# Decay row broadcast by its load, the gate kept on one partition, and a reordered schedule, in a fused RWKV and mixture-of-experts kernel

## The chip, the cores and the metric

The kernel runs on one core of one Trainium2 chip. The metric is the device time of one execution in microseconds (us); the time before is the median of three executions. Engine names in the trace: PE is TensorE's matrix multiplication, PEld its weight load, DVE is VectorE, ACT is ScalarE, POOL is GpSimd, SP is SyncE, which issues most DMAs.

## The reference

Two steps follow each other. The first is a linear attention with a decaying state, over 4 batches, 8 heads, 768 positions and a head size of 48. The second sends each whole batch through one of 8 experts.

```
# attention, for each batch and head
for t in range(S):
    y[t] = r[t] @ (state + (u*k[t])[:, None] * v[t][None, :])
    state = w[:, None] * state + k[t][:, None] * v[t][None, :]
# experts: x is y with the heads side by side, [4, 768, 384]
logits = x.mean(axis=1) @ w_gate                  # [4, 8]
e = argmax(logits); gate = softmax(logits)[e]
out[b] = gate[b] * (relu(x[b] @ w1[e[b]]) @ w2[e[b]])   # 384 -> 1024 -> 384
```

## The kernel before

The sequence is cut into blocks of 256 positions, three to a batch, so that blocks 0 to 11 cover the four batches. Instead of stepping through positions, k and r of a block are multiplied by powers of the decay (tiles `dk` and `dr`, made once at the start from `w` by a logarithm and four exponentials), and the rest is matrix products.

All the work is written as one list of tokens, ORDER. A loop at the end calls the function `do_<letter>` for each token, and each engine runs its instructions in the order in which the tokens name them. `X.2@4` means step X of block 2 in PSUM bank 4; a letter behind a slash is the engine (A for ACT, V for DVE, P for POOL, X for a product that DVE makes straight out of PSUM). Nothing is reordered at run time: an instruction that waits holds up all that stands behind it on its engine. The steps:

- L loads k, r or v of a block (on SP's queue; loads of block 7 stand back for the first part of the expert weights, those of block 8 for a later part). K and R multiply k and r by the decay, V casts v to bf16. Block 0 has K and R in two halves, the first of which is `q`.
- T transposes k and r on PE, E copies them out of PSUM, P multiplies the two (the term with u), U sums that product over a head, `v` (and `t`, a copy for POOL) multiplies it with v.
- A forms the scores on PE, G masks them on DVE (four times a block, 128x512 each). y, Y and J add the three parts of the output in PSUM: from the state, from the scores, and from the term with u.
- S adds a half block to the state in PSUM, Z decays the state, s copies it to SBUF.
- N copies the output, X transposes it for the experts (and sums it for the mean, `p`; from block 5 on `x` sums it), x copies it.
- The gate, once a batch: g (sum), l (logits on PE), m (maximum and its index on DVE), e and w (softmax), i (the index is read into a register of POOL), a and b (DMAs of the chosen expert's w1 and w2, issued by POOL).
- M and H are the first expert product and its ReLU, O and o the second and its scaling by the gate, B the store.
- `W.i.m` issues m products of 128x512 zeros that nothing reads: fillers.

Before the loop stand the load of the decay row (L129), the loads of block 0, memsets and masks. The decay row is loaded as one row on one partition; c.ln takes its logarithm there, into row 0 of a tile of zeros (`lnrow`); `cB` multiplies this tile on PE by `first`, which is one on row 0 and zero elsewhere, so that the row stands on all partitions of a PSUM bank; c.dk and c.dr (L234) make the exponentials from there. In the gate, l (L582) hands PE a column of the sums broadcast to 128x128 as the stationary operand, so that the logits stand on all partitions, and m, e and w run on 128 partitions.

S has two forms. In one (L468) it makes 16 products with 64x64 stationary operands, in the other (L477) 8 with 64x128; the former is used from block 3 on, save for the first half of a batch.

Of the kernel before, what the change touches and what calls it, by code (L numbers as in the profile page):

```python
# [757 lines left out]
```

## Time and profile before

| | |
|---|---|
| three executions | 130.01, 130.10, 130.91 us (median 130.1) |
| the profiled execution | 129.35 us, of which 127.7 us from the first to the last instruction |
| PE busy | 120.0 us |
| DVE busy | 84.7 us |
| ACT busy | 78.1 us |
| POOL busy | 78.0 us |
| HBM | 26.76 MB read, 4.72 MB written |

How to read it: the span runs from the first to the last instruction, and the time of the execution is 1.65 us longer. The profiled execution was 0.75 us shorter than the median. A share of busy time is a mean over stretches with different limits; in this kernel the stretch up to about 36 us has no expert work, and the rest has.

### The profile page before, as it was taken

The page shows a single profiled execution, that of the slowest core. Times are in us where ns is not written, and L with a number is a line of the kernel's source. Part 1 is how long each engine was busy: PE and PEld are TensorE (multiplying, and loading weights), DVE is VectorE, ACT ScalarE, POOL GpSimd, SP SyncE. Part 2 cuts the span into 40 slices and gives each one's busy share as a digit, 9 for nine tenths or more (in the row PEclk, how much of TensorE's full clock was granted, in tenths as well). Part 3 has the DMA queues.
Part 4 walks back from the last instruction along what each step waited for, and adds up shares of the span by engine and source line. Part 5 has one row for each costly group of instructions (what it writes and reads, how often), then busy time and mean ns, then how long its engine had stood idle before and what let it go on. Part 6 is the DMA issues. An engine that isn't in the chain of part 4 may idle for free.

```text
span 127.7 us, 4933 instructions
## 1 busy us (share of the span) xinstructions
PE 120.0 (94%) x2103; PEld 82.1 (64%) x2107; DVE 84.7 (66%) x192; ACT 78.1 (61%) x192; POOL 78.0 (61%) x72
## 2 busy tenths in 40 slices
...
GB/s 28 324 320 325 322 234 314 189 243 270 129 139 276 224 161 232 277 258 236 229 270 280 273 224 90 62 185 197 64 0 0 9 174 202 240 400 211 0 257 115
DMA packets 47768, 25.50 MB, mean 200 GB/s; under 512 B 38401, under 2 KB 46338, under 8 KB 47746
## 3 DMA queue, kind: packets, MB, share of 16 engines
...
q8 instruction: 16, 0.26, 0.8%
q14 instruction: 6, 0.05, 0.1%
HBM read 26.76 MB, written 4.72 MB: 246 GB/s over the span
## 4 chain that ended last, share of the span: by engine, by line
PE 91%; ACT 2%; DVE 2%; issue 2%; ACTq 0%
PE hp L648 25%; PE op L683 24%; PE y L500 8%; PE at L439 5%; PE wp L219 5%; PE tp L325 4%; PE tp L338 3%; PE xp L538 3%; PE s L468 3%; PE s L477 2%; PE lgp L582 2%; PE y L425 2%; PE u L399 2%; PE lnb L226 1%; PE op L673 1%
## 5 line engine op out<-in xcount | busy, mean ns | idle before, releaser
L648 PE MATMUL hp<-xt,w 128*128 128x384 bf16 x192 | 36.3, 326 | 0.0
L683 PE MATMUL op<-w,ht 128*128 128x384 bf16 x184 | 33.7, 326 | 0.0
L449 DVE TENSOR_TENSOR gt<-at,mask 128x512 bf16<-128x512 f32 x48 | 31.0, 683 | 3.8 <-PE at L439 3.5
L663 DVE TENSOR_SCALAR ht<-hp 128x384 bf16<-128x384 f32 x30 | 16.0, 552 | 13.3 <-PE hp L648 13.3
L683 PEld LDWEIGHTS <-ht 128*128 128x128 bf16 x184 | 17.4, 99 | 10.8 <-issue 0.2
L648 PEld LDWEIGHTS <-w 128*128 128x128 bf16 x192 | 17.4, 98 | 10.3 <-issue 0.3
L294 POOL TENSOR_TENSOR kp<-k,dk 128x768 bf16<-128x768 f32 x11 | 20.0, 1818 | 2.7 <-DMA k<-in_k_dram 2.1
L661 ACT ACTIVATE ht<-hp 128x384 bf16<-128x384 f32 x34 | 15.5, 501 | 9.4 <-PE hp L648 9.4
L294 POOL TENSOR_TENSOR rp<-r,dr 128x768 bf16<-128x768 f32 x11 | 20.0, 1814 | 1.6 <-DMA r<-in_r_dram 1.5
L704 ACT ACTIVATE ob<-op,gw 128x384 f32<-128x384 f32 (+1 forms) x17 | 9.5, 576 | 13.1 <-PE op L683 11.0
L627 POOL DMA_DIRECT2D w<-in_moe_w_dram x9 | 7.2, 797 | 15.7 <-issue 10.4
L365 ACT COPY tw<-tp 128x1024 bf16<-128x1024 bf16 x12 | 12.2, 1016 | 5.2 <-PE tp L338 4.6
L389 POOL TENSOR_TENSOR prod<-tw 128x1024 bf16<-128x1024 bf16 x6 | 12.7, 2121 | 1.8 <-DVE tw L363 1.8
L210 ACT CAST xn<-y 128x384 bf16<-128x384 f32 x22 | 9.7, 486 | 5.6 <-PE y L425 5.6
L706 DVE TENSOR_SCALAR ob<-op,gw 128x384 f32<-128x384 f32 (+1 forms) x8 | 4.6, 590 | 11.4 <-PE op L683 8.0
L495 ACT CAST st<-s 64x192 bf16<-64x192 f32 x32 | 10.1, 314 | 3.5 <-PE s L477 2.2
L219 PE MATMUL wp<-zeros 128*128 128x512 bf16 x30 | 9.0, 413 | 1.5 <-DVE zeros L135 1.4
L439 PE MATMUL at<-tw 64*64 64x128 bf16 x384 | 9.7, 219 | 0.4 <-DVE tw L363 0.2
L559 ACT ACTIVATE xt<-xp 128x256 bf16<-128x256 bf16 x21 | 7.8, 391 | 3.1 <-PE xp L538 3.1
L210 ACT CAST vb<-v 128x768 bf16<-128x768 f32 x10 | 8.4, 840 | 1.5 <-DMA v<-in_v_dram 1.5
L363 DVE COPY tw<-tp 128x512 uint32<-128x512 uint32 x12 | 8.1, 687 | 1.7 <-PE tp L338 0.8
L416 DVE TENSOR_TENSOR vt<-vb,u 128x768 bf16<-128x768 bf16 x8 | 7.6, 947 | 1.6 <-PE u L399 1.6
...
## 6 DMA issues: line engine op xcount, KB each, us to landing
w<-in_moe_w_dram POOLq DMA_DIRECT2D x15, 384.0 KB, 6.5
k<-in_k_dram SPq DMA_DIRECT2D x12, 384.0 KB, 5.2
r<-in_r_dram SPq DMA_DIRECT2D x12, 384.0 KB, 5.4
v<-in_v_dram SPq DMA_DIRECT2D x12, 384.0 KB, 5.9
out_dram<-ob SPq DMA_DIRECT2D x11, 384.0 KB, 6.9
w<-in_moe_w_dram POOLq DMA_DIRECT2D x2, 192.0 KB, 4.6
...
out_dram<-ob SPq DMA_DIRECT2D x1, 192.0 KB, 2.2
```

The lines of the kernel that those rows point to most:

```text
L210: nc.scalar.copy(out, in_)
L219: nc.tensor.matmul(out=wp, lhsT=zeros[:, 0:128], rhs=zeros, start=True, stop=True)
L294: e.tensor_mul(dst[n % NR].rearrange("p (g a) d -> p a g d", a=2)[:, :, :, 0:D], *(t.rearrange("p (a q) j d -> p a (q j) d", a=2) for t in ...
L365: nc.scalar.copy(out, in_)
L389: e.tensor_mul(prod.rearrange("x g c p -> x c g p"), tk, tw[:, :, 1].rearrange("x c q j p -> x c (q j) p"))
L439: nc.tensor.matmul(out=at[a][64 * c : 64 * c + 64, 128 * q : 128 * q + 128], lhsT=tw[rows, c, 0, q, j, :], rhs=tw[rows, c, 1, q].rearrange ...
L449: nc.vector.tensor_mul(gts[n][:, j, a], ats[n, j][a].rearrange("x (q s) -> x q s", q=NQ), mask[:, j].rearrange("x j p -> x (j p)").unsquee ...
L500: nc.tensor.matmul(out=out, lhsT=lhsT, rhs=rhs, start=(n, c) not in begun, stop=False, skip_group_check=True)
L648: nc.tensor.matmul(out=hp[:, 0:SB], lhsT=wts[b][1][i][:, ct, 128 * f : 128 * f + 128], rhs=xts[b][:, ct, SB * sb : SB * sb + SB], start=(c ...
L661: nc.scalar.activation(out=o, in_=hp[:, 0:SB], func=ACT.Relu)
L663: nc.vector.tensor_scalar_max(o, hp[:, 0:SB], 0.0)
L683: nc.tensor.matmul(out=op[:, 0:DM], lhsT=hts[b, half][:, f, 128 * si : 128 * si + 128], rhs=wts[b][2][half][:, f, :], start=(half == 0 and ...
```

## The change

The row of the decay is loaded with a DMA that reads it 128 times, once for each partition, and the logarithm is taken on all of them (`lnw`); `cB` and the memset of `lnrow` are gone, and c.dk and c.dr read SBUF. The logits are formed on one partition; m, e and w run there, and m reads PSUM without a copy. Two new steps bring the gate's weight to all partitions: f, a product on PE of a row of ones with the weight, and h, a copy of its result. S and J take their form from a letter in the token: Q is the form with small stationary operands, H for J writes 128 columns. `ident` becomes the middle of a tile with zeros on both sides.

ORDER is new as a whole. 47 fillers stand in it instead of 34, of which 34 instead of 20 follow the first transpose of block 0. Many copies change their engine: of `v` 11 are on DVE instead of 8 (and the copy `t` is gone), of N 6 instead of 2, of s 8 instead of 4, of o 10 instead of 8, of x 3 instead of 1, of E 13 instead of 12, of H 24 instead of 30; POOL casts five v instead of two. S is in its 16-product form 11 times instead of 12. Loads are spread over the list; on SP's queue only the gate's matrix (cg), the order within some blocks and the stores move.

The list up to the first expert product, and from l.3 to the first product of the last batch, before (-) and after (+); the rest of the list is left out:

```diff
-W.99.4@0 L.k.0 L.r.0 L.v.0 L.k.1 L.r.1 L.v.1 L.k.2 L.r.2 L.v.2 c.ln/A cB@0 c.dk.0/A c.dk.1/A W.33.2@1 W.15.2@2
-q.k/P K.0/V K.1/P c.dr.0/A c.dr.1/A W.13.2@3 W.14.4@4 q.r/V R.0/V T.0.1@5 E.0.1/V V.0/A cT@6 T.0.0@1 E.0.0/V
-S.0.0 W.35.2@2 ct/A P.0/X A.0.0@03 A.0.1@46 G.0.0.1/V G.0.0.0/V G.0.1.0/V s.0.1/A cu/P R.1/P S.0.1 cw/A K.2/P
-Z.1/V R.2/P U.0@1 T.1.0@2 W.29.6@5 V.1/A E.1.0/A T.1.1@3 s.1.0/A S.1.0 s.1.1/A t.0/A G.0.1.1/V L.k.3 L.r.3
-L.v.3 V.2/A E.1.1/V P.1/X A.1.1@04 A.1.0@25 G.1.0.1/V G.1.1.1/V T.2.0@6 S.1.1 Z.2/V E.2.0/A y.0.1@3 W.23.2@5
-v.0/P U.1@4 T.2.1@5 L.k.4 G.1.1.0/V Y.0@6 G.1.0.0/V y.1.0@1 y.1.1@0 s.2.0/A S.2.0 v.1/V Y.1 J.0 E.2.1/A
-A.2.0@24 N.0.1/A N.0.0/A P.2/X K.3/P G.2.0.1/V G.2.0.0/V J.1 N.1.0/A N.1.1/A R.3/P L.r.4 L.v.4 A.2.1@53
-G.2.1.0/V X.0@6 G.2.1.1/V V.3/A U.2@4 s.2.1/A T.3.0@1 p.0/V T.3.1@2 E.3.1/A X.1@0 E.3.0/V v.2/V p.1/V P.3/X
-K.4/P y.2.1@5 S.3.0 s.3.1/A y.2.0@3 Y.2 J.2 N.2.0/A A.3.1@14 S.3.1 T.4.0@2 R.4/P x.1/A N.2.1/V Z.4/V G.3.1.0/V
-X.2@3 E.4.0/A L.r.5 cg p.2/V g.0/V y.3.1@5 T.4.1@0 l.0@1 V.4/P G.3.1.1/V s.4.0/A m.0/V A.3.0@24 x.2/A x.0/A
-E.4.1/A L.k.5 G.3.0.0/V G.3.0.1/V S.4.0 s.4.1/A W.2.4@1 U.3@3 v.3/V W.24.2@2 Y.3@6 e.0/A R.5/P L.r.6 A.4.0@14
-A.4.1@23 P.4/X i.0/P S.4.1 a.0.q/P L.v.5 J.3 G.4.0.1/V G.4.1.0/V G.4.1.1/V G.4.0.0/V N.3.1/A N.3.0/A W.37.4@0
-L.k.6 y.4.0@4 L.v.6 X.3@5 V.5/A U.4@0 K.5/P T.5.0@62 y.4.1@3 a.0.0/P T.5.1 Z.5/V p.3/A x.3/A Y.4 M.0.2.1@1
+W.99.9@0 L.k.0 L.r.0 L.v.0 V.0/P L.k.1 L.r.1 c.ln/A c.dk.0/A c.dk.1/A q.k/V K.0/V K.1/P c.dr.0/A c.dr.1/A
+W.15.2@0 W.6.2@1 T.0.0@2 W.0.4@3 q.r/V R.0/V T.0.1@4 E.0.0/V E.0.1/V P.0/X W.5.4@5 L.v.1 cT@6 A.0.1@01 S.0.0
+s.0.1/A G.0.1.0/V ct/V A.0.0@32 W.21.4@5 G.0.0.1/V G.0.1.1/V cu/P S.0.1/Q W.30.4@4 cw/A Z.1/V s.1.0/A
+G.0.0.0/V L.k.2 cg U.0@0 y.0.1@6 R.1/P T.1.0@2 E.1.0/A v.0/V T.1.1@5 W.14.2@1 W.26.2@4 L.r.2 L.v.2 E.1.1/V
+P.1/X Y.0@3 A.1.0@01 J.0/Q V.1/P L.k.3 A.1.1@24 S.1.0/Q N.0.0/A G.1.0.0/V G.1.0.1/V L.r.3 y.1.0@5 s.1.1/A
+N.0.1/A K.2/P U.1@3 T.2.0@0 E.2.0/A R.2/P V.2/P G.1.1.1/V G.1.1.0/V S.1.1/H y.1.1@1 v.1/V L.v.3 T.2.1@6 Z.2/V
+Y.1 L.r.4 X.0@4 K.3/P E.2.1/A R.3/P L.k.4 J.1/Q A.2.0@20 N.1.0/A s.2.0/A p.0/A x.0/A P.2/X W.8.2@3 G.2.0.1/V
+A.2.1@56 G.2.1.0/V S.2.0/H y.2.0@3 U.2@0 G.2.0.0/V T.3.0@5 G.2.1.1/V N.1.1/A s.2.1/A T.3.1@4 E.3.1/A X.1@2
+y.2.1@1 V.3/A E.3.0/V R.4/P Y.2 v.2/V A.3.0@65 p.1/A J.2/H S.3.0 T.4.1@0 P.3/X N.2.1/V x.1/V N.2.0/A X.2@4
+U.3@3 W.36.2@1 K.4/P s.3.1/A p.2/A x.2/A G.3.0.1/V g.0/V L.v.4 V.4/A G.3.0.0/V l.0@2 m.0/V A.3.1@51 S.3.1/Q
+G.3.1.0/V i.0/P a.0.q/P Z.4/V G.3.1.1/V T.4.0@4 L.k.5 E.4.1/A v.3/V E.4.0/A e.0/A W.16.6@6 y.3.1@5 L.r.5
+s.4.0/A Y.3@1 P.4/X A.4.1@64 J.3/Q L.v.5 A.4.0@23 N.3.0/A a.0.0/P K.5/P N.3.1/A S.4.0/H s.4.1/A L.r.6 L.k.6
+R.5/P G.4.1.1/V G.4.1.0/V w.0/V U.4@0 X.3@1 W.11.2@4 L.v.6 G.4.0.1/V G.4.0.0/V L.k.7 y.4.1@5 f.0@6 W.25.2@4
+y.4.0@3 S.4.1/H T.5.0@42 T.5.1 L.r.7 Y.4 h.0/A p.3/V v.4/V x.3/V V.5/A M.0.2.0@6 M.0.2.1@0 M.0.3.1@1 E.5.1/V
...
-M.2.2.1@2 H.2.2.1/V o.1.5/V M.2.4.0@1 O.1.0.1 l.3@5 O.1.4.0@4 M.2.6.0@2 M.2.0.1@6 H.2.4.0/A H.2.0.1/A m.3/V
-M.2.4.1@1 H.2.4.1/V O.2.1.0@5 O.2.2.0@6 O.2.4.0@1 O.1.4.1 H.2.6.0/A H.2.5.0/A O.2.5.0@2 O.2.3.0@0 o.1.0/V
-O.2.2.1 o.2.2/A O.2.3.1 O.2.0.0@3 o.2.3/A B.2.1 B.1.0 O.2.1.1 O.2.5.1 o.1.4/A i.3/P a.3.0/P M.3.0.0@6 o.2.5/V
+g.3/V H.2.1.1/V H.2.3.1/V f.2@3 M.2.5.1@5 H.2.6.0/A l.3@2 M.2.5.0@1 h.2/A H.2.5.0/A O.1.4.1 b.2.1/P b.2.0/P
+m.3/V o.1.4/A e.3/A O.2.0.0@3 M.2.6.1@0 H.2.6.1/A H.2.2.1/A O.2.1.0@1 M.2.7.1@6 H.2.5.1/V H.2.7.1/A O.2.4.0@5
+O.2.5.0@2 O.2.2.0@0 O.2.3.0@4 O.2.0.1 O.2.2.1 O.2.4.1 O.2.1.1 o.2.4/A o.2.0/A i.3/P a.3.1/P M.3.6.0@6
```

The rest of the change:

```diff
@@ -125,16 +126,15 @@
         return dma
 
 
-    wrow = const.tile([1, DM], FP32, tag="wrow", name="wrow")
-    nc.sync.dma_start(out=wrow, in_=w.rearrange("h d -> (h d)").unsqueeze(0))
+    wrow = const.tile([128, DM], FP32, tag="wrow", name="wrow")
+    nc.sync.dma_start(out=wrow, in_=w.rearrange("h d -> (h d)").partition_broadcast(128))
     nc.scalar.preload_act_table_set("natural_log_exp_and_others")
     load(k, "k", 0)
     load(r, "r", 0)
     load(v, "v", 0)
     zeros = const.tile([128, 512], BF16, tag="zeros", name="zeros")
     nc.vector.memset(zeros, 0.0)
-    lnrow = const.tile([128, DM], FP32, tag="lnrow", name="lnrow")
-    nc.vector.memset(lnrow, 0.0)
+    lnw = const.tile([128, DM], FP32, tag="lnw", name="lnw")
     first = const.tile([128, 128], FP32, tag="first", name="first")
     nc.vector.memset(first, 0.0)
     nc.vector.memset(first[0:1, :], 1.0)
@@ -157,8 +157,10 @@
     nc.gpsimd.memset(unit8, 0.0)
     nc.gpsimd.affine_select(out=unit8, in_=unit8, compare_op=ALU.not_equal, fill=1.0,
                             base=0, pattern=[[-1, 2 * NQ]], channel_multiplier=1)
-    ident = const.tile([128, HP], BF16, tag="ident", name="ident")
-    nc.gpsimd.memset(ident, 0.0)
+
+    wide = const.tile([128, 3 * HP], BF16, tag="ident", name="ident")
+    ident = wide[:, HP : 2 * HP]
+    nc.gpsimd.memset(wide, 0.0)
     for c in range(2):
         t = ident[64 * c : 64 * c + 64]
         nc.gpsimd.affine_select(out=t, in_=t, compare_op=ALU.not_equal, fill=1.0,
@@ -219,19 +221,12 @@
             nc.tensor.matmul(out=wp, lhsT=zeros[:, 0:128], rhs=zeros, start=True, stop=True)
 
 
-    logs = []
-
-    def do_cB(eng, bk):
-        lnb = bank(bk[0], "lnb")
-        nc.tensor.matmul(out=lnb[:, 0:DM], lhsT=first, rhs=lnrow, start=True, stop=True)
-        logs.append(lnb)
-
     def do_c(eng, bk, what, j=0):
         if what == "ln":
-            nc.scalar.activation(out=lnrow[0:1, :], in_=wrow, func=ACT.Ln)
+            nc.scalar.activation(out=lnw, in_=wrow, func=ACT.Ln)
         else:
             t, col = (dk, col_k) if what == "dk" else (dr, col_r)
-            nc.scalar.activation(out=t[:, :, j, :], in_=logs[0][:, 0:DM].rearrange("p (h d) -> p h d", h=H),
+            nc.scalar.activation(out=t[:, :, j, :], in_=lnw.rearrange("p (h d) -> p h d", h=H),
                                  func=ACT.Exp, scale=col[:, j : j + 1])
 
 
@@ -422,8 +417,10 @@
         for c in range(2):
             for j in range(2):
                 rows = slice(64 * c, 64 * c + 64)
+                half = eng == "H"
                 nc.tensor.matmul(
-                    out=ys[n][c][64 * j : 64 * j + 64, 0:DM], lhsT=ident[rows, :],
+                    out=ys[n][c][:, 0:DM] if half else ys[n][c][64 * j : 64 * j + 64, 0:DM],
+                    lhsT=wide[rows, HP - 64 * j : 3 * HP - 64 * j] if half else ident[rows, :],
                     rhs=vt[rows, j].rearrange("p h d -> p (h d)"),
                     start=False, stop=True, skip_group_check=True,
                 )
@@ -452,16 +449,13 @@
             mask[:, j].rearrange("x j p -> x (j p)").unsqueeze(1).to_broadcast([128, NQ, 128]),
         )
 
-
-    QUARTERS = 3
-
     def do_S(eng, bk, n, c):
         b, blk = divmod(n, NB)
         if blk == 0 and c == 0:
             sps[b] = bank(7, f"s{b}")
         sp = sps[b]
         rows = slice(64 * c, 64 * c + 64)
-        if n >= QUARTERS and (blk or c):
+        if eng == "Q":
             for q in range(NQ):
                 for j in range(2):
                     for a in range(2):
@@ -574,42 +568,50 @@
         nc.vector.reduce_sum(sums, pooleds[b], axis=AX.X)
         gates[b] = sums
 
+
     def do_l(eng, bk, b):
         sums = gates[b]
         lgp = bank(bk[0], f"lgp{b}")
         gates[b] = (sums, lgp)
         for ct in range(NCT):
-            nc.tensor.matmul(
-                out=lgp[:, 0:E], lhsT=sums[:, ct : ct + 1].to_broadcast([128, 128]),
-                rhs=wg[:, ct, :], start=(ct == 0), stop=(ct == NCT - 1),
-            )
+            nc.tensor.matmul(out=lgp[0:1, 0:E], lhsT=sums[:, ct : ct + 1], rhs=wg[:, ct, :],
+                             start=(ct == 0), stop=(ct == NCT - 1))
 
     def do_m(eng, bk, b):
         lgp = gates[b][1]
-        lg = buf("lg", b, [128, E], FP32, 4)
-        nc.vector.tensor_copy(lg, lgp[:, 0:E])
-        top8 = buf("top8", b, [128, 8], FP32, 4)
+        lg = lgp[0:1, 0:E]
+        top8 = buf("top8", b, [1, 8], FP32, 4)
         nc.vector.max(out=top8, in_=lg)
-        idx8 = buf("idx8", b, [128, 8], U32, 4)
+        idx8 = buf("idx8", b, [1, 8], U32, 4)
         nc.vector.max_index(out=idx8, in_max=top8, in_values=lg)
-        negmax = buf("negmax", b, [128, 1], FP32, 4)
+        negmax = buf("negmax", b, [1, 1], FP32, 4)
         nc.vector.tensor_scalar_mul(negmax, top8[:, 0:1], -1.0 / S)
         gates[b] = (lg, negmax)
         idxs[b] = idx8
 
     def do_e(eng, bk, b):
         lg, negmax = gates[b]
-        exps = buf("exps", b, [128, E], FP32, 4)
+        exps = buf("exps", b, [1, E], FP32, 4)
         nc.scalar.activation(out=exps, in_=lg, func=ACT.Exp, bias=negmax[:, 0:1], scale=1.0 / S)
         gates[b] = exps
 
     def do_w(eng, bk, b):
         exps = gates[b]
-        ssum = buf("ssum", b, [128, 1], FP32, 4)
+        ssum = buf("ssum", b, [1, 1], FP32, 4)
         nc.vector.reduce_sum(ssum, exps, axis=AX.X)
-        gw = buf("gw", b, [128, 1], FP32, 4)
+        gw = buf("gw", b, [1, 1], FP32, 4)
         nc.vector.reciprocal(gw, ssum)
         gates[b] = gw
+
+    def do_f(eng, bk, b):
+        gwp = bank(bk[0], f"gwp{b}")
+        nc.tensor.matmul(out=gwp[:, 0:1], lhsT=first[0:1, :], rhs=gates[b], start=True, stop=True)
+        gates[b] = gwp
+
+    def do_h(eng, bk, b):
+        gwp = gates[b]
+        gates[b] = buf("gwc", b, [128, 1], FP32, 4)
+        copy(eng, gates[b], gwp[:, 0:1])
 
     def do_i(eng, bk, b):
         idx8 = idxs[b]
```

## Rows read from the trace of the kernel before

**Rows 1.** Windows (us): busy of PE, PEld, DVE, ACT, POOL; clock, DMA share, GB/s

```profile
3.40:4.40 1.00, 1.00 (x2) 0.59 (x3) 0.92 (x6) 0.00 (x0) 0.95 (x3) 1.00 1.17 325
7.67:36.02 28.35, 26.30 (x688) 20.86 (x693) 25.29 (x55) 21.11 (x45) 24.19 (x18) 1.00 1.03 255
36.02:95.28 59.26, 59.26 (x1214) 41.27 (x1214) 44.95 (x91) 40.27 (x112) 45.62 (x32) 1.00 0.94 196
36.02:124.20 88.18, 88.14 (x1401) 59.31 (x1400) 54.32 (x115) 52.27 (x142) 48.72 (x36) 1.00 0.84 184
40.00:44.00 4.00, 4.00 (x100) 2.89 (x99) 4.00 (x8) 3.31 (x7) 3.45 (x4) 1.00 1.15 263
```

**Rows 2.** The chain that ended last: start us, us, what

```profile
1.38 1.89 PE wp L219 x4
3.37 1.55 PE lnb L226 x2
...
9.46 0.44 PE s L477 x8
...
19.54 0.32 PE y L425 x4
...
25.53 0.24 PE s L468 x16
...
27.43 0.84 PE lgp L582 x6
...
31.75 0.73 issue
...
36.02 1.57 PE hp L648 x9
...
97.39 0.57 PE lgp L582 x6
```

**Rows 3.** Timeline of the opening: start us, us, engine, line, operation [idle before it]

```profile
2.46 0.52 ACT L231 ACTIVATE lnrow<-wrow 1x384 f32<-1x384 f32 x1 [0.26 <-DMA wrow<-in_w_dram]
...
4.74 2.32 PE L219 MATMUL wp<-zeros 128*128 128x512 bf16 x10
...
5.01 1.05 ACT L234 ACTIVATE dk<-lnb,col_k 128x384 f32<-128x384 f32 x2 [2.02 <-PE lnb L226]
...
6.09 1.05 DVE L286 TENSOR_TENSOR kp<-k,dk 128x384 bf16<-128x384 f32 x1 [1.31 <-ACT dk L234]
...
7.07 1.01 DVE L286 TENSOR_TENSOR rp<-r,dr 128x384 bf16<-128x384 f32 x2
...
7.67 0.23 PE L325 MATMUL tp<-unit,rp 128*128 128x128 bf16 x1 [0.60 <-DVE rp L286]
```

**Rows 4.** DMA issues of k of block 0 (issued at 1.33): KB, us to landing

```profile
k<-in_k_dram SPq DMA_DIRECT2D x1, 384.0 KB, 3.5
```

**Rows 5.** Groups of instructions by shape: busy us, mean ns | idle before

```profile
L663 DVE TENSOR_SCALAR ht<-hp 128x384 bf16<-128x384 f32 x30 | 16.0, 552 | 13.3 <-PE hp L648 13.3
...
L416 DVE TENSOR_TENSOR vt<-vb,u 128x768 bf16<-128x768 bf16 x8 | 7.6, 947 | 1.6 <-PE u L399 1.6
...
L399 PE MATMUL u<-U,prod 128*128 128x8 bf16 x96 | 4.2, 167 | 0.1
...
L582 PEld LDWEIGHTS lgp<-wg,sums 128*128 128x128 f32 x24 | 3.1, 189 | 0.3
```

**Rows 6.** Timeline, gates of batches 0 and 3: index found, weights issued

```profile
28.79 0.16 DVE L594 FIND_INDEX8 idx<-top,lg 128x8 uint32<-128x8 f32 x1
...
30.50 0.81 POOL L627 DMA_DIRECT2D w<-in_moe_w_dram  x1 [2.81 <-DVE gt L449]
...
99.95 0.80 POOL L627 DMA_DIRECT2D w<-in_moe_w_dram  x1 [10.42 <-issue]
```

**Rows 7.** DMA issues of the window 30 to 31, then of 99.9 to 100.3

```profile
w<-in_moe_w_dram POOLq DMA_DIRECT2D x1, 192.0 KB, 4.5
...
w<-in_moe_w_dram POOLq DMA_DIRECT2D x1, 384.0 KB, 5.2
```

More of the change, by code (lines that the diff above doesn't have):

```diff
@@ new lines @@
+T.6.1 M.0.1.1@5 X.4@3 M.0.0.1@2 s.5.1/A H.0.1.0/A H.0.1.1/A E.6.0/V G.5.1.1/V U.5@6 H.0.0.1/A M.0.0.0@0
+y.5.0@5 y.5.1@1 M.0.4.0@2 H.0.4.0/A p.4/V Y.5 H.0.0.0/A L.v.7 E.6.1/V S.6.0 A.6.1@42 v.5/V x.4/V J.5/Q P.6/P
+N.5.0/A M.0.5.0@6 G.6.1.0/V M.0.6.1@3 G.6.1.1/V H.0.5.0/V N.5.1/A X.5@0 x.5/A M.0.7.1@5 M.0.5.1@4 H.0.5.1/A
+H.0.6.1/A M.0.4.1@1 s.6.1/V L.r.8 U.6@2 L.k.8 M.0.7.0@6 H.0.7.1/A g.1/V l.1@0 M.0.6.0@4 H.0.4.1/V m.1/V
+H.0.7.0/A S.6.1/H Z.7/V K.7/P R.7/P T.7.0@31 A.6.0@56 G.6.0.0/V L.r.9 T.7.1 H.0.6.0/A y.6.1@4 e.1/A O.0.1.0@0
@@ new lines @@
+O.0.4.0@5 G.6.0.1/V v.6/V E.7.0/V L.v.8 E.7.1/A s.7.0/V O.0.1.1 O.0.2.0@6 i.1/P a.1.0/P O.0.4.1 O.0.2.1
+o.0.1/A V.7/A w.1/V f.1@1 h.1/V o.0.2/V o.0.4/A K.8/P A.7.0@23 S.7.0/Q G.7.0.0/V T.8.0@05 Y.6@1 s.7.1/A R.8/P
+T.8.1 a.1.1/P b.1.0/P P.7/P R.9/P G.7.0.1/V A.7.1@62 J.6/Q L.k.9 N.6.1/V S.7.1/Q L.r.10 O.0.0.0@3 L.v.9
+N.6.0/A X.6@1 L.k.10 x.6/A V.8/A E.8.0/V O.0.0.1 O.0.5.0@4 U.7@0 G.7.1.1/V G.7.1.0/V Z.8/V s.8.0/A o.0.0/V
+E.8.1/V K.9/P M.1.1.1@2 M.1.2.0@6 H.1.2.0/A v.7/V O.0.5.1 A.8.1@13 o.0.5/V A.8.0@56 H.1.1.1/A G.8.0.1/V
@@ new lines @@
+H.1.4.0/V H.1.4.1/V H.1.6.0/A H.1.7.1/A O.1.0.0@2 U.9@5 X.8@3 M.1.5.1@1 v.9/V T.10.0@04 x.8/A g.2/V K.11/P
+S.9.0 T.10.1 T.11.0@65 l.2@3 s.9.1/V R.11/P m.2/V E.10.1/A S.9.1/Q O.1.0.1 Z.10/V H.1.5.1/V E.10.0/V O.1.1.0@4
+y.9.1@1 T.11.1 Y.9@0 V.10/P o.1.0/A e.2/A s.10.0/V i.2/P a.2.0/P S.10.0/Q E.11.0/A J.9/Q A.10.0@23 O.1.1.1
+M.1.6.1@6 E.11.1/A L.v.11 O.1.3.0@5 a.2.1/P P.10/P G.10.0.1/V o.1.1/V s.10.1/V G.10.0.0/V B.0.1 B.0.2
+O.1.2.0@3 P.11/P N.9.0/V H.1.6.1/A O.1.3.1 o.1.3/A V.11/A S.10.1/Q A.10.1@46 U.10@2 G.10.1.1/V O.1.2.1
```

51 lines of the change are left out of this document (18 added, 33 removed).

## The prediction

> **What bounds the kernel now.** I read the windows first. From 36.02 us, where the first expert product starts, to 124.20 us PE is busy for 88.14 of 88.18 us [rows 1]: behind that point every us of PE work, added or removed, is a us of the result, and no other engine matters unless it makes PE wait. After 124.20 only the last scaling and the last store follow, and the change leaves them as they are. From the first transpose at 7.67 to 36.02 PE is busy for 26.30 of 28.35 us, so it stands for 2.05 us [rows 1], and part of its busy time is 20 fillers, which give nothing. Ahead of 7.67 nothing useful is done on PE. The granted clock reads 1.00 in all these windows [rows 1], full speed (2.4 GHz), so there is no slow clock behind 7.67 that more fillers could cure.
>
> Next I read the chain and the timeline of the opening. The logarithm starts at 2.46, when the row of `w` has landed; the spreading product on PE takes 1.55 from 3.37 [rows 2, 3]; the exponentials of dk start at 5.01, two in 1.05; the products of k run on DVE at 6.09 and of r at 7.07; the first transpose is at 7.67 [rows 3]. k of block 0, issued at 1.33, lands 3.5 later, at 4.83 [rows 4], so it waits for dk, not the other way round.
>
> Last I read the gate of batch 0: its index is written at 28.95, POOL issues the first weights at 30.50, and 4.5 later they are there, at 35.0 [rows 6, 7], 1.0 ahead of the first product that needs them.
>
> The account is therefore: the end is the time of the first useful product, plus the useful PE work, plus fillers behind it, plus PE's waits behind it.
>
> **The start.** The new load writes 128 rows of 1.5 KB, 0.197 MB, ahead of k on SP's queue, and every later load stands behind it. In the opening the loads run at 325 GB/s [rows 1], by which it takes 0.60. The logarithm then starts near 3.06 and takes 0.52 as before, since dk's operations on 128 partitions take no longer than that for the same 384 elements; dk is done after another 1.05 [rows 3], at 4.65. k lands at 4.83 + 0.60 = 5.43 and is now the later of the two. Both halves of k go to DVE. The pair of r took 1.01 [rows 3], while the half of k that ran on DVE beside POOL's half took 1.05; with POOL away from it I take 1.05 for both. They end near 6.5, and the first transpose follows at 6.6, 1.1 earlier than now. The 13 fillers ahead of it do not hold it up: the first four take 1.89 from 1.38, ten later ones 2.32 from 4.74 [rows 2, 3]; eight at 0.45, slow until then, and five at 0.22 end near 6.1. No row shows a broadcast load. Bounds: it costs nothing, as the one row does (first product at 6.0), or as much as a whole 0.39 MB load, 1.2 (7.2). So **-1.1, from -1.7 to -0.5**; I take the rate of the rows, because the pieces go through the same queue.
>
> **Fillers.** 34 stand behind the first transpose instead of 20. Ten took 2.32, some 0.22 apart [rows 3]: 14 x 0.216 = **+3.0**. They are issued whether PE would wait there or not.
>
> **Waits.** The fillers stand where PE would otherwise wait, so the 2.05 shrinks. I walked the new order of PE, DVE, ACT and POOL to the first expert product with these durations. DVE has about 1.4 more in the opening (v of block 0, 0.95 [rows 5], one x, less the small copies of p and of the logits) and begins 1.1 earlier, so it is level with now. What remains on PE are eight waits of 0.05 to 0.35, the longest for v of block 2, 1.25 in all: **-0.8**. Of the 2.05 now, some 1.15 are two pieces that wait for nothing seen (0.73 at 31.75 [rows 2], 0.42 at 22.71); if they come back on top, the term is +0.35; if all waits vanish, -2.05.
>
> **The gate's products.** Four l steps take 0.84, 0.57 [rows 2], and of the two others one 0.75 and one 0.57: 2.7. Their weight loads of 128 fp32 columns take 189 ns each [rows 5]. The new ones load one column. No row shows that; the nearest has eight products of 8 columns in each u step, 96 in 4.2 us of busy time [rows 5], 44 ns each, so six take 0.26: **-1.7**, from 0 (the load costs the same) to -2.3 (0.1 each). The new f is one fp32 product on a 128-column operand. An l step issues six pairs for three products, two passes each, in 0.57, so f is 0.19: 4 x 0.19 = **+0.8**, from 0.4 (one pass) to 1.1 (at the pace of 0.84). The copy h hides behind expert products; without that cover it would hold o by some 0.2 a batch.
>
> For a load of one column the Trainium skill has a price, in TensorE: Matmul & The Clock Gate, section LDWEIGHTS: the time goes with the number of columns, and not with the contraction. By its figure the load itself would be about a nanosecond, and an l step, by the floor of 25 ns a product in its section "Wait — 56ns, not 53.3ns?", an estimated 0.15; the sum would then be 0.4 lower. No row here shows a one-column load.
>
> **S and J.** The 8-product form takes 0.44, the 16-product one 0.24 [rows 2]; one more step has the former: +0.2. J of block 2 goes to 128 columns; J takes 0.32 [rows 2], and I add half of it: +0.15, from 0 to 0.3.
>
> **What costs nothing.** Running m, e and w on one partition doesn't shorten them by rows, and the copy of the logits that goes is not late: the weights land 1.0 ahead. The moves between ACT, DVE and POOL are covered by PE behind 36.02. For the last batch the cover shrinks: from l to its first expert product stand 53 products of 384 columns, 8.6 at 0.163 apiece (1.57 for nine with the first one's latency [rows 2]). Now weights are issued at 99.95, 2.0 after l ends at 97.96, and land 5.2 later [rows 2, 6, 7], 7.2 after l: 1.4 to spare. On SP's queue the first store moves ahead of four loads and makes them wait for two o steps of batch 0; they feed blocks 10 and 11, and I put that at nothing; the cover is several us of expert products.
>
> **Sum.** -1.1 + 3.0 - 0.8 - 1.7 + 0.8 + 0.35 = +0.55. Against the profiled execution's 129.35 that is 129.9. It lies 0.75 under the median, so the forecast is **130.6**, no change that can be told; its own range is 129.8 to 131.3.
>
> **Rivals.** *The fillers are free.* DVE is busy for 25.29 of 28.35 us in the opening [rows 1]; if it and the weights set the first expert product, PE's extra fillers only fill its waits. Then that product comes when the weights allow, at 35.1 (-0.9), and behind it three l save 1.1, three f cost 0.6, one S 0.2: -1.2, and 128.9. With a broadcast that delays no load the gate comes 0.6 sooner: 128.3. I take 128.6. For it: the load on DVE. Against: in the walk PE, not DVE, is last at the first expert product, by 0.8.
>
> *DVE becomes the bound.* DVE gets three more v at 0.95 and, net, eight more operations near 0.55 [rows 5]: 7.2, of which 5.2 behind 36.02. There it is busy for 44.95 of 59.26 us until the last block is done, but 4.00 of 4.00 from 40 to 44 [rows 1], and over 3.7 in three more such windows. PE then waits for scores to be masked and PSUM banks to come free. It decides from where the work bunches: spread evenly there is room; if a third of it falls into full stretches, 1.7 are lost: 132.3. For it: ACT, which gives the work up, had less to do there (40.27 [rows 1]). Against: 50 of 59 us is still not full.
>
> *The broadcast does not do what it says.* If reading one row 128 times costs 1.2 beyond my upper end, the first product is no earlier than now; with 1.1 back in the sum, 131.7.
>
> **How the numbers follow.** Forecast 0.47, free fillers 0.28, DVE 0.14, broadcast 0.11. About 1% is what a measurement here can tell from no change: 128.8 and 131.4. Faster: 0.25 of the free fillers and 0.02 of the forecast's low tail, 0.27. Slower: DVE and broadcast, less 0.02 that stays under the line, and 0.03 of the forecast: 0.26. Same: 0.47. The range goes from inside the free fillers to the price of DVE: 128.4 to 132.3.
>
> **What would show it.** Right: first transpose near 6.6; first expert product near 36.6; PE unbroken from there; l under 0.3 each and f near 0.2. Free fillers: first expert product before 35.5. DVE: gaps on PE between 40 and 95 that end with a masking or a copy on DVE. Broadcast: the logarithm starting after 4, k landing after 6.5. The forecast is wrong above all if the waits that fillers stand in for are misjudged, or the pieces that wait for nothing seen come in other numbers.

## The result and the profile after

After the change an execution takes 130.83 us (median of 22 runs, 129.90 to 132.29); the kernel before, run beside it, 130.06 (22 runs, 128.97 to 132.87). The ratio is 1.0067, 95% interval 1.0044 to 1.0090: 0.7% slower, less than the 1% that the prediction takes as the line to no change, though the interval leaves out 1. The ratios, here and below, leave out single slow executions, so they are not quite the quotients of the medians. The forecast was 130.6. The profiled execution took 130.28 us with a span of 128.7, against 129.35 and 127.7 before; what follows accounts for that 1.0 us of span.

The windows of the kernel after, cut at its own first transpose, its first expert product, the end of the last block's stretch and the end of PE's work, answer to [rows 1]. Columns: window, length, then busy us and instructions of PE, PEld, DVE, ACT and POOL, granted clock of PE, DMA share, GB/s.

```profile
7.11:36.58 29.47, 28.95 (x708) 21.67 (x708) 28.32 (x58) 19.39 (x44) 23.29 (x19) 1.00 1.03 256
36.58:96.36 59.78, 59.55 (x1208) 40.96 (x1209) 48.09 (x99) 36.66 (x98) 44.42 (x31) 1.00 0.97 204
36.58:125.37 88.79, 88.53 (x1398) 58.66 (x1398) 57.12 (x122) 49.05 (x129) 47.41 (x35) 1.00 0.85 186
```

The account by stretches: to the first transpose 7.11 instead of 7.67 (-0.56); from there to the first expert product 29.47 instead of 28.35 (+1.12); from there to the end of PE's work 88.79 instead of 88.18 (+0.61); the tail 3.33 instead of 3.50 (-0.17). Sum +1.0. In the opening DVE is now busy for 28.32 of 29.47 us; it was 25.29 of 28.35. Behind 36.58 PE stands for 0.26 us in all, and DVE has 11.7 us to spare up to 96.36.

The timeline of the opening after (start, us, engine, line, operation; in brackets the idle time before it and what ended that) answers to [rows 3]:

```profile
0.94 0.38 SPq L130 DMA_DIRECT2D wrow<-in_w_dram  x1
1.39 4.79 PE L221 MATMUL wp<-zeros 128*128 128x512 bf16 x13 [1.39 <-DVE zeros L136]
5.06 0.52 ACT L226 ACTIVATE lnw<-wrow 128x384 f32<-128x384 f32 x1 [2.85 <-DMA wrow<-in_w_dram]
5.69 1.12 ACT L229 ACTIVATE dk<-lnw,col_k 128x384 f32<-128x384 f32 x2
6.50 1.03 DVE L281 TENSOR_TENSOR kp<-k,dk 128x384 bf16<-128x384 f32 x2 [2.12 <-DMA k<-in_k_dram]
7.11 0.23 PE L320 MATMUL tp<-unit,kp 128*128 128x128 bf16 x1 [0.93 <-DVE kp L281]
```

The loads issued there, with the time from issue to landing, answer to [rows 4]:

```profile
k<-in_k_dram SPq DMA_DIRECT2D x1, 384.0 KB, 5.0
wrow<-in_w_dram SPq DMA_DIRECT2D x1, 192.0 KB, 4.1
```

The row, issued at 0.94, is there 4.1 later, and the logarithm starts at 5.06, 2.6 later than before [rows 3]. k, issued at 1.38, takes 5.0 instead of 3.5 [rows 4] and lands at about 6.4; DVE's product with dk follows at once. The first transpose still comes 0.56 earlier, and that is the new order's doing, as the experiments show: DVE makes both halves of k first, and PE transposes k first (`kp`), 0.61 after that product starts, where the kernel before transposed r first and waited for its product at 7.07 [rows 3].

The chain that ended last in the kernel after, from block 2 to the first expert product (start, us, what), answers to [rows 2]:

```profile
22.14 1.46 DVE gt L446 x3
...
25.39 0.74 DVE prod L381 x2
...
27.11 0.60 DVE gt L446
...
28.77 0.47 POOLq L618
...
30.27 6.26 DMA w<-in_moe_w_dram
36.58 1.64 PE hp L650 x9
```

Before, PE led most of this chain up to the first expert product. Now DVE leads it from 22.14, then the gate and POOL's queue, then the load of the weights, which takes 6.3 us instead of 4.5 [rows 7]; their issue at 30.27 is only 0.23 earlier than before [rows 6].

The groups of the gate's products (busy us, mean ns of one), which answer to [rows 5], and one l step and one f step from the chain:

```profile
L577 PE MATMUL lgp<-wg,sums 128*1 128x8 f32 x24 | 1.2, 169 | 0.0
L577 PEld LDWEIGHTS lgp<-wg,sums 128*1 128x1 f32 x24 | 0.8, 81 | 1.1 <-DVE sums L568 0.4 <-ACT gwc L212 0.3 <-issue 0.3
```

```profile
49.30 0.23 PE lgp L577 x6
...
55.74 0.31 PE gwp L608 x2
```

Those means are of single pipelined instructions; what counts is the step, 0.23 for six products and 0.31 for f's two.

### The profile page after: what moved, and what is told of

Read it like the earlier page. It is cut to its first block, busy times and chain, and to the rows that moved or that the text cites. A ratio compares the mean times of both kernels' runs of the same rounds, so it can differ in the third digit from the quotient of the medians.

```text
span 128.7 us, 4946 instructions
## 1 busy us (share of the span) xinstructions
PE 122.2 (95%) x2118; PEld 81.9 (64%) x2118; DVE 89.6 (70%) x201; ACT 71.7 (56%) x176; POOL 74.9 (58%) x71
## 4 chain that ended last, share of the span: by engine, by line
PE 79%; DMA 9%; DVE 6%; issue 2%; ACT 1%; POOLq 1%; SPq 0%; DVEq 0%
PE hp L650 25%; PE op L685 24%; PE y L494 6%; DMA w<-in_moe_w_dram 5%; PE at L436 5%; PE wp L221 4%; DMA k<-in_k_dram 4%; PE xp L532 3%; PE s L462 2%; PE tp L320 2%; DVE gt L446 2%; PE tp L333 2%; PE y L421 2%; PE u L394 1%; PE s L471 1%
## 5 line engine op out<-in xcount | busy, mean ns | idle before, releaser
L650 PE MATMUL hp<-xt,w 128*128 128x384 bf16 x192 | 36.9, 326 | 0.2 <-DMA w<-in_moe_w_dram 0.2
L663 ACT ACTIVATE ht<-hp 128x384 bf16<-128x384 f32 x40 | 18.5, 494 | 12.4 <-PE hp L650 12.3
L665 DVE TENSOR_SCALAR ht<-hp 128x384 bf16<-128x384 f32 x24 | 12.5, 550 | 13.5 <-PE hp L650 13.4
L706 ACT ACTIVATE ob<-op,gwc 128x384 f32<-128x384 f32 x15 | 8.4, 582 | 14.6 <-PE op L685 10.2
L221 PE MATMUL wp<-zeros 128*128 128x512 bf16 x47 | 13.7, 420 | 1.4 <-DVE zeros L136 1.4
L360 ACT COPY tw<-tp 128x1024 bf16<-128x1024 bf16 x11 | 11.0, 1016 | 3.1 <-PE tp L333 2.4
L212 ACT CAST xn<-y 128x384 bf16<-128x384 f32 x18 | 8.3, 480 | 6.9 <-PE y L421 6.5
L489 ACT CAST st<-s 64x192 bf16<-64x192 f32 x24 | 7.5, 312 | 6.4 <-PE s L471 3.5
L411 DVE TENSOR_TENSOR vt<-vb,u 128x768 bf16<-128x768 bf16 x11 | 10.4, 943 | 0.1
L708 DVE TENSOR_SCALAR ob<-op,gwc 128x384 f32<-128x384 f32 (+1 forms) x10 | 5.5, 571 | 5.8 <-PE op L685 3.9
L436 PEld LDWEIGHTS <-tw 64*64 64x64 bf16 x384 | 7.0, 106 | 1.8 <-issue 1.1
```

The lines of the kernel that those rows point to most:

```text
L360: nc.scalar.copy(out, in_)
L411: e.tensor_mul(vt.rearrange("p j h d -> p h j d"), vbs[n], col.rearrange("p j h -> p h j").unsqueeze(3).to_broadcast([128, H, 2, D]))
L436: nc.tensor.matmul(out=at[a][64 * c : 64 * c + 64, 128 * q : 128 * q + 128], lhsT=tw[rows, c, 0, q, j, :], rhs=tw[rows, c, 1, q].rearrange ...
L650: nc.tensor.matmul(out=hp[:, 0:SB], lhsT=wts[b][1][i][:, ct, 128 * f : 128 * f + 128], rhs=xts[b][:, ct, SB * sb : SB * sb + SB], start=(c ...
L663: nc.scalar.activation(out=o, in_=hp[:, 0:SB], func=ACT.Relu)
L665: nc.vector.tensor_scalar_max(o, hp[:, 0:SB], 0.0)
```

## Experiments

The diffs show the lines that matter, and the rest of each edit is left out. Each run has a ratio to the kernel before on the same chip; where two are set against each other, it is these ratios that are compared. "First expert product" is the start of the first M; it was 35.96 in a record of before (its window above begins at 36.02), and the last group of O products started at 123.33, 87.37 behind it. In the kernel after these are 36.58 and 124.51, 87.93 apart. These times come from one profiled execution of each kernel.

**One row again.** The kernel after, with the load of one row and the spreading product of the kernel before; the fillers ahead of the first transposes are redealt to keep the banks free.

```diff
-W.99.9@0 L.k.0 L.r.0 L.v.0 V.0/P L.k.1 L.r.1 c.ln/A c.dk.0/A ...
-W.15.2@0 W.6.2@1 T.0.0@2 W.0.4@3 q.r/V ...
+W.99.4@0 L.k.0 L.r.0 L.v.0 V.0/P L.k.1 L.r.1 c.ln/A cB@3 c.dk.0/A ...
+W.15.5@0 W.6.4@1 T.0.0@2 W.0.4@5 q.r/V ...
```

> The changed kernel with the decay row loaded once, on one partition, and spread by the product on PE as before; 13 fillers still stand ahead of the first transpose. Theory (the broadcast costs more at the start than the product did, since it lands late and holds back every load behind it): the logarithm starts near 2.5 instead of 5.06, k of block 0 lands near 4.8 instead of 6.38, the first transpose comes near 6.7 instead of 7.11, and the time falls by 0.3 to 1.0 us against the changed kernel, to about 130.1. Rival (the broadcast is worth its product): the spreading product and its round trip return, the first transpose is at 7.7 and the time rises by 0.5, to 131.3.

Measured: 129.92 us (12 runs), ratio 1.0027, interval 0.9994 to 1.0061; span 128.1. The timeline of its opening:

```profile
2.42 0.52 ACT L234 ACTIVATE lnrow<-wrow 1x384 f32<-1x384 f32 x1 [0.21 <-DMA wrow<-in_w_dram]
3.07 1.57 PE L229 MATMUL lnb<-lnrow,first 128*128 128x384 f32 x2
4.43 2.47 PE L222 MATMUL wp<-zeros 128*128 128x512 bf16 x9
4.74 1.05 ACT L237 ACTIVATE dk<-lnb,col_k 128x384 f32<-128x384 f32 x2 [1.80 <-PE lnb L229]
5.35 1.03 DVE L289 TENSOR_TENSOR kp<-k,dk 128x384 bf16<-128x384 f32 x2 [0.57 <-ACT dk L237]
6.74 0.61 PE L328 MATMUL tp<-unit,kp 128*128 128x128 bf16 x8
```

With the product of 1.57 on the path, dk still starts at 4.74 instead of 5.69, and the transposes follow at 6.74. They now wait for the nine fillers ahead of them and no longer for k, whose product starts at 5.35. The first expert product comes at 35.48, 1.1 earlier than in the kernel after, and PE leads the chain up to it; the last group of O products comes at 123.99, 0.5 earlier. So in the new order the broadcast load seems to cost more than the product that it replaces, by the medians about 0.4%. The two intervals overlap, so the total alone does not show it; the trace points the same way, and the old order, next, shows it clearly. At 42.79 PE then stands for 0.83, for nothing that the trace names, which eats much of the 1.1.

**The broadcast alone**, in the kernel before, with cB gone.

```diff
-... L.v.2 c.ln/A cB@0 c.dk.0/A c.dk.1/A W.33.2@1 ...
+... L.v.2 c.ln/A c.dk.0/A c.dk.1/A W.33.2@1 ...
-    nc.sync.dma_start(out=wrow, in_=w.rearrange("h d -> (h d)").unsqueeze(0))
+    nc.sync.dma_start(out=wrow, in_=w.rearrange("h d -> (h d)").partition_broadcast(128))
```

> The kernel before with the broadcast load alone, the spreading product and its bank gone. Theory (the load lands late, at about 5.05, and k of block 0 at 6.4 instead of 4.83): the products of k end near 7.4 instead of 7.14, those of r near 8.7 instead of 8.08, and the time is 0.2 to 0.7 over the kernel before, about 130.6. Rival (as predicted, the start comes 1.1 earlier): 129.0.

Measured: 132.40 us (6 runs), ratio 1.0197 (1.0133 to 1.0261). From its page, PE's busy tenths and its granted clock in 40 slices of 3.27 us:

```profile
PE   5939989999799999999999999999999999999980
PEclk9985699999999999999999999999999999999999
```

and from its timeline the first transposes:

```profile
8.53 0.23 PE L317 MATMUL tp<-unit,rp 128*128 128x128 bf16 x1 [2.02 <-DVE rp L278]
...
10.06 1.03 PE L317 MATMUL tp<-unit,kp 128*128 128x128 bf16 x8
```

PE stands for 2.02 us before the first transpose, in a slice where it is busy for three tenths, and in the slices behind it the granted clock is 0.5 to 0.6, about the lower of its two levels (1.2 of 2.4 GHz). Eight transposes then take 1.03, against 0.61 in the run above at full clock. The first expert product comes at 38.92. So the late row costs twice in this order: by the wait, and by the clock that falls behind it.

Together with the run before this gives the first transpose in all four cases: old order 7.67 with one row and 8.53 with the broadcast, new order 6.74 and 7.11. In the old order the broadcast moves it 0.86 later; with the broadcast in both, the new order moves it 1.42 earlier. The 6.74 hangs on the pace of the fillers (7.70 in the last run below, with the same opening), so for the new order it is the start of DVE's product of k that compares: 5.35 with one row, 6.50 with the broadcast.

**The broadcast alone, with nine more fillers** in front of the first transpose.

```diff
-... c.dr.0/A c.dr.1/A W.13.2@3 W.14.4@4 q.r/V ...
+... c.dr.0/A c.dr.1/A W.13.2@3 W.14.13@4 q.r/V ...
```

> The kernel before with the broadcast load alone, and nine more fillers ahead of the first transpose, so that PE does not stand from 6.5 to 8.5 us. Theory (of the 2.5 us that the broadcast alone cost, the late landing is some 0.9 at the first transpose, and the rest is PE at half its clock for 8 us after the wait): the clock stays at full speed, transposes of 8 take 0.55 and not 0.96, and the time is 130.5 to 131.2. Rival (the late landing costs all of it): 132 or more.

Measured: 131.32 us (6 runs), ratio 1.0128 (1.0079 to 1.0176), just above the theory's range. Its page has the clock whole:

```profile
PEclk9999999999999999999999999999999999999999
```

The first expert product comes at 36.18. By the medians the clock was some 0.7% of the 2.0%; the intervals overlap, so the size is uncertain, though the two rows show that the clock fell in the one kernel and not in the other. Behind that product this kernel needs 88.60 to the last O group, 1.2 more than the kernel before, 0.5 of it a wait for the expert weights.

**What makes the load slow.** Two kernels, each the kernel before with one more load of 192 KB into a tile that nothing reads, ahead of k: once the row of w 128 times, once 128 different rows of v.

```diff
+    nc.sync.dma_start(out=spare, in_=w.rearrange("h d -> (h d)").partition_broadcast(128))
```

```diff
+    nc.sync.dma_start(out=spare, in_=v[3].rearrange("h s d -> (h s d)")[0 : 128 * DM].rearrange("(p x) -> p x", x=DM))
```

> The kernel before, which keeps its one-row load, with one more load of 0.197 MB that nobody reads ahead of k of block 0: the decay row 128 times. If reading one row 128 times is what is slow, this load takes some 4 us to land and k lands near 6.3 instead of 4.83. If the late landing in the changed kernel came from elsewhere, k lands near 5.4.

> As the run with the same row, but the added load reads 128 different rows of 1.5 KB, the same number of bytes and pieces. If reading one row is the slow part, this one lands within 3 us and k near 5.4 (0.6 for 0.197 MB at 325 GB/s). If the cost is that of any such load ahead of k, k lands near 6.3 again.

One execution each (131.48 and 130.13 us). The DMA issues, first of the kernel that reads one row, then of the one that reads 128:

```profile
k<-in_k_dram SPq DMA_DIRECT2D x1, 384.0 KB, 5.2
spare<-in_w_dram SPq DMA_DIRECT2D x1, 192.0 KB, 4.5
```

```profile
k<-in_k_dram SPq DMA_DIRECT2D x1, 384.0 KB, 3.5
spare<-in_v_dram SPq DMA_DIRECT2D x1, 192.0 KB, 2.4
```

Same bytes, same pieces, same place in the queue: 4.5 us against 2.4. And k, issued at 1.74 in both, comes 5.2 or 3.5 later; 3.5 is what it takes with no more than the one row ahead of it [rows 4]. So the price is not for 192 KB: 128 different rows delay k by the later issue alone (0.4). What differs is that one load reads the same row 128 times; it also reads w where the other reads v, and no run reads one row of v 128 times.

**No fillers** behind the first transpose, in the kernel after: 34 products out.

```diff
-W.15.2@0 W.6.2@1 T.0.0@2 W.0.4@3 q.r/V ... W.5.4@5 ... W.21.4@5 ... W.30.4@4 ... W.14.2@1 W.26.2@4 ...
-... W.8.2@3 ... W.36.2@1 ... W.16.6@6 ... W.11.2@4 ... W.25.2@4
+W.15.2@0 W.6.2@1 T.0.0@2 q.r/V ...
```

> The changed kernel without the 34 fillers behind the first transpose; the 13 ahead of it stay. Theory of the prediction (each filler costs its 0.216 us less the waits it fills, +3.0 - 0.8 against 20): all of them cost at least 2, and the time falls to 128.8 or lower. Rival (the fillers are free, since VectorE, busy for 28.3 of 29.5 us in the opening, and the first weights set the first expert product): it stays within 0.3 us of 36.6, and the time is 130.5 to 131.1. A third outcome: PE's clock falls in the gaps, and the time rises by 1 or more.

Measured: 131.62 us (6 runs), ratio 1.0122 (1.0047 to 1.0197). Its page and its timeline:

```profile
PE   5956898997989989999999999999999999999990
PEclk9998559999999999999999999999999999999999
```

```profile
14.66 1.04 PE L319 MATMUL tp<-unit,rp 128*128 128x128 bf16 x8 [0.34 <-POOL rp L288]
```

Neither side held, and the third outcome came: PE is busy for five and six tenths in the slices from 6.5 to 13 us, the granted clock then falls to half, and stays there until about 19 us. Eight transposes take 1.04 there. The first expert product comes at 37.15, 0.57 later than with the fillers. In the total the rise over the kernel after is about 0.5% by the ratios, and the intervals overlap.

**Twenty fillers** instead of 34.

```diff
-... W.0.4@3 ... W.5.4@5 ... W.21.4@5 ... W.30.4@4 ... W.14.2@1 ... W.16.6@6
+... W.0.2@3 ... W.5.2@5 ... W.21.2@5 ... W.30.2@4 ... W.16.2@6
```

> The changed kernel with 20 fillers behind the first transpose instead of 34, as many as the kernel before has. Theory of the prediction (+3.0 for 14 fillers less 0.8 of waits): the time falls by 1.5 to 2.2, to 128.8. Rival (the opening is set by VectorE and the weights, the fillers stand in waits): within 0.4 of the changed kernel, 130.4 to 131.1, first expert product at 36.3 to 36.7. Third outcome: the clock falls as it did without any, and the time rises to 131.2 or more.

Measured: 130.56 us (12 runs), ratio 1.0062 (1.0036 to 1.0088), as the kernel after. Its first stretch, in the same window as above:

```profile
7.11:36.58 29.47, 26.88 (x693) 20.46 (x694) 27.79 (x58) 19.23 (x44) 23.00 (x19) 1.00 1.06 265
```

PE is busy for 2.07 us less, its first expert product comes at the same 36.58, and the clock stays at 1.00. So these 14 fillers are free here, and PE's work does not set this stretch. Which engine does is read from chains only: in this run the chain goes over loads and POOL's products of k and r up to 19.3, over PE to 22.45, over DVE to 28.1, and last over a load of k and POOL's product of r, behind which come the last transposes, a y step and the first expert product:

```profile
28.39 5.46 DMA k<-in_k_dram
...
34.01 1.79 POOL rp L289
```

In the run with one row PE leads the chain, so whether the fillers are free there no run shows.

**The gate on one partition alone**, in the kernel before (the copy of the logits kept), with f and h in banks that are free shortly after w.

```diff
+... s.5.1/V G.5.0.1/V f.0@5 h.0/A X.4@3 M.0.1.1@2 ...
+... M.1.7.1@4 X.6@3 f.1@6 h.1/V x.6/A ...
-        lhsT=sums[:, ct : ct + 1].to_broadcast([128, 128]), out=lgp[:, 0:E]
+        lhsT=sums[:, ct : ct + 1], out=lgp[0:1, 0:E]
```

> The kernel before with the gate on one partition alone (the copy of the logits kept, at 1x8; f and h stand between the gate's weight and its first use). Theory (behind 36 us each us of PE work is a us of the result): an l step falls from 0.57 to 0.84 to 0.23, f adds 0.31 each, so PE gets 0.5 to 0.6 less and the time is about 129.5. Rival (f waits for the softmax and holds up PE): one or more waits of 0.3 on PE in front of f, and 130.1 or more.

Measured: 130.59 us (11 runs), ratio 1.0095 (1.0062 to 1.0127). PE's waits in it (line, waited for: us, times, longest):

```profile
PE s L420 <- issue: 1.0, 1, 1.0
...
PE gwp L566 <- DVE gt L401: 0.7, 2, 0.4
PE y L452 <- issue: 0.5, 1, 0.5
```

The rival held: f waits for a bank that DVE is still masking from, and all of PE stands behind it. The first expert product is 0.5 earlier (35.42), the last O group 1.8 later (125.17); f's waits are 0.7 of this.

**The same with f in spare columns of the state's bank**, so that it waits for no other use of a bank. (The 1.2 in the expectation is not in the trace: there the two waits are 0.3 and 0.4.)

```diff
-        gwp = bank(bk[0], f"gwp{b}")
+        gwp = sps[max(sps)][:, DM + 64 :]
```

> The kernel before with the gate on one partition as in the run of the gate alone, but f writes into spare columns of the bank that holds the state, so that it waits for no bank. Theory (in the first run of the gate PE waited for f's bank, 0.3 at block 5 and 1.2 at block 8, both ended by a masking on VectorE): these waits go, l saves 1.8 in all and f costs 1.2, and the time is 0.3 to 0.8 under the kernel before, about 129.4. Rival (f's own cost, and what the shorter l steps exposed, ate the gain): 130.2 or more.

Measured: 130.82 us (9 runs), ratio 1.0092 (1.0055 to 1.0130): that theory fell. In its chain f (L566, under the name of the state's tile) comes behind DVE's copy of the masked state out of the same bank:

```profile
37.37 1.25 DVE gt L401 x2
38.62 0.48 DVE st L449
39.14 0.38 PE s L566 x2
```

**The same with f just ahead of the first O of its batch**, where its cover is largest.

```diff
-... a.1.1/P b.1.1/P O.0.5.0@4 E.7.1/V O.0.4.0@1
+... a.1.1/P b.1.1/P f.0 O.0.5.0@4 h.0/A E.7.1/V O.0.4.0@1
```

> The kernel before with the gate on one partition, f in spare columns of the state's bank and directly ahead of the first O of its batch, where PE has a long run of expert products. Theory (the two earlier runs of the gate lost to the place of f): f costs 0.31 a batch and no wait, the sum with l is -0.5, and the time is about 129.3. Rival (f's cost is more than its 0.31, wherever it stands): 130.2 or more.

Measured: 132.23 us (6 runs), ratio 1.0197 (1.0151 to 1.0244): that theory fell too. PE's waits in it:

```profile
PE lgp L582 <- DVE tw L363: 0.8, 1, 0.8
PE at L439 <- issue: 0.4, 1, 0.4
PE u L399 <- POOL prod L389: 0.4, 1, 0.4
PE s L614 <- DVE s L487: 0.4, 1, 0.4
```

Its first expert product is the earliest of all (34.33), 1.6 ahead of the kernel before, but the last O group is 1.75 later: 90.75 apart instead of 87.37. PE gets ahead, and then waits, in part for what DVE and POOL have not made.

**Logits on one partition without f and h**, in the kernel before; the output is scaled by the constant 0.5 instead of the gate.

```diff
-        gates[b] = gw
+        gates[b] = half_gate
```

> The kernel before with l, m, e and w on one partition and without f and h: the output is scaled by a constant 0.5 instead of the gate's weight, so that part of the computation is left out. Theory (each us of PE work behind 36 us is a us of the result): l shortens by 0.5 to 0.6 at the first gate and by 1.2 in the three others, and the time falls by 1.2 to 1.8, to about 128.4. Rival (PE's order stands ready behind other engines, so that a shorter l only lengthens waits): less than 0.6 gained, 129.3 or more.

Measured: 132.61 us (6 runs), ratio 1.0185 (1.0134 to 1.0235): the theory fell as to the total, and the loss lies where neither side looked, ahead of the first expert product. Its chain, and a window of it:

```profile
24.22 5.02 DMA wg<-in_moe_w_gate_dram
29.24 0.14 issue
29.38 0.36 PE lgp L584 x6
...
33.22 2.19 issue
```

```profile
36.00:38.00 2.00, 2.00 (x9) 0.90 (x10) 0.54 (x3) 1.59 (x3) 1.50 (x2) 0.50 1.18 161
```

The gate's matrix lands at 29.24, and l.0 runs at 29.38, 1.95 later than before [rows 2]; from 3 to 10 us the DMA engines moved 268 GB/s here and 321 in the kernel before. PE then stands 2.19 inside an S step, and the granted clock falls to 0.50. The ten fillers behind cB took 3.84 instead of 2.32 [rows 3], and the first transpose came at 8.46. No line of the edit touches those loads or fillers; why they are slow stays open. Behind its first expert product (40.35) the kernel needs 86.82 to the last O group, 0.55 less than before, of the 1.2 that three short l steps without f save.

**The old gate in the new order**: the kernel with one row again, and the gate on 128 partitions without f and h.

```diff
-... y.4.1@5 f.0@6 W.25.2@4
-... T.5.1 L.r.7 Y.4 h.0/A p.3/V ...
+... y.4.1@5 W.25.2@4
+... T.5.1 L.r.7 Y.4 p.3/V ...
```

> The changed kernel with the one-row load and spreading product, as in the first experiment, and the gate of before as well (l on 128 partitions, no f and h): only the new order, the forms of S and J and the moved copies are left of the change. Theory (l saves 1.7 in all, f costs 1.2 where it stands): 0.3 to 0.7 slower than the run with the one-row load, 130.4. Rival (f and h cost as much as l saves): the same, 129.6 to 130.2.

Measured: 130.57 us (12 runs), ratio 1.0037 (1.0006 to 1.0068), against 1.0027 with the new gate: no difference that can be told. In the new order the gate on one partition, with its f and h, shows neither gain nor cost. The two profiled executions cannot be set against each other: the nine fillers behind cB took 3.52 us here and 2.47 there, so the first transpose came at 7.70 and not at 6.74, with the same opening. No kernel of the study is shown to be faster than the one before.

## Why the prediction was right

The total (130.6 for 130.83) and the first expert product (36.6 for 36.58) came out as forecast, but by luck, through errors that cancel: the first transpose came 0.5 later than the 6.6 forecast, and the stretch behind it took 29.47 instead of 30.0. The 36.6 is not even what the prediction's own terms give: -1.1 + 3.0 - 0.8, the first l (-0.6), the first f (+0.2) and J (+0.15) make 36.9.

**The start** was mis-sized: -0.56 instead of -1.1, just inside the dear one of its bounds (-0.5). The step that failed is "I take the rate of the rows, because the pieces go through the same queue". The load took 4.1 us from issue to landing, and k came near 6.4 instead of 5.43. The dummy loads show why: 128 different rows behave as the step assumed, the same row 128 times doesn't. k came 1.0 late, but the first transpose only 0.5, because the 6.6 waits for both halves of k; the first transpose follows DVE's first product by 0.6, before [rows 3] as after, which from 5.43 gives 6.0. That the direction still held is not due to the product that went: with the broadcast alone the first transpose comes later than before (8.53), and with the product back in the new order DVE has k at 5.35 and not at 6.50. It is due to the new order, k first. The rival "does not do what it says" had the mechanism (logarithm after 4: 5.06) without its whole price; k stayed just under its mark of 6.5.

**Fillers and waits** (+3.0 and -0.8) failed as a way of counting. The stretch grew by 1.12, but not from PE's work: with 14 fillers less it has the same length. DVE, busy for 28.32 of 29.47 us, leads the end of the chain, and then the weights take 6.3 instead of 4.5. So the rival "the fillers are free" had the mechanism in that PE's fillers cost nothing, and its time (128.6) failed on the gate: it let the weights be there at 35.1, and they were there at 36.5. What the walk had wrong is the sentence "DVE ... is level with now". From just before DVE's first product with dk to the first expert product, before and after, the windows are:

```profile
4.80:36.02 31.22, 28.57 (x699) 21.69 (x702) 26.87 (x57) 23.59 (x49) 25.77 (x20) 1.00 1.04 261
4.40:36.58 32.18, 30.68 (x715) 22.16 (x713) 28.94 (x59) 21.34 (x47) 24.38 (x21) 1.00 1.04 261
```

DVE's busy time grew by 2.1, which is nearly the 1.4 forecast and the second half of k (0.55). But its first product came at 6.50, 0.4 later than before [rows 3], and did not begin 1.1 earlier; so it was not level, and the gate's chain ends on it. The remark that no slow clock is left for fillers to cure was true of the kernel before and didn't carry over: in the new order, without any, the clock falls. With 20 of them it stayed at 1.00.

**The gate's products**: the first l step took 0.30, the other three 0.23 each, 0.99 for 2.73, so -1.74 for -1.7. By the floor in the Trainium skill, TensorE: Matmul & The Clock Gate, section "Wait — 56ns, not 53.3ns?", I had estimated 0.15 a step; the trace has 0.23, 38 ns a product, so the nearest row of the profile was the better guide. The load of one column, estimated there at about a nanosecond, stands with 81 ns, against 189 for 128 columns [rows 5]. f was mis-sized: 0.31 each instead of 0.19, +1.24 for +0.8.

**Behind the first expert product** -0.3 was forecast and +0.61 came: l -1.2, three f +0.93, one more S in eight products +0.2, which is -0.07; PE's waits +0.22 (0.26 of 88.79 for 0.04 of 88.18). The remaining 0.46 I could not assign to single steps; it is in PE's busy time, in which the pipelined records' modelled ends are counted. The prediction's "every us of PE work, added or removed, is a us of the result" did not hold where PE got ahead: with the gate alone the first expert product came earlier (34.33, 35.14, 35.42), and the time behind it grew to 90.75, 89.01 and 89.75. There PE stood for 2.1, 0.8 and 1.3 us in all, against 0.04 before; the rest of the growth is in its busy time and is not explained.

**DVE as the bound** did not come in the kernel after (48.09 of 59.78, with PE at 59.55), but waits for DVE and POOL took back a part of the earlier start in the three kernels with the gate alone (1.6, 0.7 and 0.7 us, in the order above).

**What costs nothing** held for h and for the last batch. For f the prediction counted PE's time alone and no wait. That held in the new order; in the old one the gate with it cost 0.9% in one place, in either bank, and 2.0% in another.
